# Top-32 attention and an ELU feed-forward layer: nine transposes of a step in a row, one GpSimd operation for both rows' distances, and three-tile feed-forward blocks split into one and two tiles

## The chip, the core and the metric

The kernel runs on one core of a Trainium2 chip. The metric is the device time of one launch in microseconds (us), the median of several runs. A core has a matrix engine (TensorE, PE in the profile; PEld is its loading of weights), VectorE (DVE), ScalarE (ACT), GpSimd (POOL) and a queue that issues DMAs (SyncE, SP). Each engine takes its instructions in program order, and instructions of different engines wait for each other by semaphores.

## The reference

```python
scores = scale * np.matmul(q, k.transpose(0, 1, 3, 2))      # 8 batches, 8 heads, 576 x 576, head_dim 64
kth = np.partition(scores, -top_k, axis=-1)[..., -top_k:-top_k + 1]   # top_k = 32
scores = np.where(scores >= kth, scores, -1000000000.0)
scores = scores - np.max(scores, axis=-1, keepdims=True)
attn = np.exp(scores)
attn = attn / (np.sum(attn, axis=-1, keepdims=True) + 1e-09)
attn_out = np.matmul(attn, v)
# (B,H,S,D) -> (B*S, H*D): x has 4608 tokens of 512
h = x @ w_in                                                 # 512 -> 2048
g = np.where(h > 0.0, h, np.exp(np.minimum(h, 0.0)) - 1.0)
out = g @ w_out                                              # 2048 -> 512
```

So there are two parts: attention in which each query keeps its 32 largest scores, and a feed-forward layer (FFN) on the tokens that come out of it. All of it is computed in fp32.

## The kernel before

**Steps.** The 576 queries of a batch are four tiles of 128 and a remainder of 64. A step is one query tile with a pair of heads ("two rows": head i=0 and i=1, each 128 queries by 576 keys); for the remainder it is 64 queries with four heads. There are 18 steps in a batch, 144 in all. In an even batch the order is tiles (0,1), tiles (2,3), remainder; in an odd batch the remainder comes first, so that the remainders of a pair of batches, which together fill one tile of 128 tokens, follow each other. The first eight steps (`n < tight`) are ordered by a scheduler, while the weights are still being decoded; from step 8 on the order is the one written out in the main loop (L702 to L755), which in step n works on four steps at once:

- at its head the score matmuls of step n+2 (`scores`, matmuls at L331; ScalarE copies them out at L339), then the attention matmuls of a group of two steps that has all its transposes (`attend`, L470, with the copy to the FFN's input `xT` at L497);
- in four parts, the selection of step n on VectorE (`select`: `max` at L373 and L385, `match_replace` at L378), 14 passes of 576 elements over two rows;
- between the parts, for step n-1: the distance of the 32nd score from the largest on GpSimd (L406), and on ScalarE a Prelu and an Exp that leave exp(score - largest) for the kept scores and 0 for the others (`mask`, L407 and L408, row 0 after the first part, row 1 after the second); after the fourth part the division by the sum on GpSimd (`normalise`, L418 to L425);
- for step n-2: nine 128x128 transposes on TensorE (`turn`, L444) with three copies by ScalarE (L445). `main` (chunks 0 to 3) and `rest` (chunk 4, which holds parts of both rows) come after the second part, `other` (chunks 5 to 8) after the third;
- four times in a step `feed(n, 0.25)` puts in pieces of the FFN.

`turn(done, main)` needs row 0 of `normalise`, `rest` and `other` need row 1. `main` and `other` each take one of two PSUM buffers of `ps_t`, which `attend` uses too; `rest` uses a corner of the scores' own PSUM tile.

**FFN blocks.** Tiles of a pair of batches are put together to blocks of tokens (L604 to L613). The first pair has five blocks of one tile and two of two; each later pair has blocks (0,1), (2,3), (rest,4,5), (6,7), where `rest` is the tile of the two remainders. A block of s tiles has 16 pieces `hidden(f)` of four matmuls with 128·s columns (L545), then 4·s pieces `project` of four matmuls with 512 columns (L573). A `hidden` fills PSUM banks of 512 columns: one f for three tiles (384 of 512), two for two tiles, four for one. Each is evicted by two Relus (L555, L558), then an Exp and a copy on ScalarE (L560, L564), and an addition on GpSimd, or on VectorE in early steps and in the last block (`close_gates`, L515 and L517). An fp32 matmul of the program is two records in the profile.

**How much FFN a step gets.** A list `due` has for each block the step at which its input is ready (for a block, that of its last tile) and the planned cost of all blocks before it (`HIDDEN`, L21, per `hidden` by block size, and `PROJECT`). `feed` takes the smallest slope from what has been fed to any later entry of `due`:

```python
        ahead = [(w - fed["sum"]) / (x - fed["at"]) for x, w in due if x > fed["at"]]
        if ahead:
            fed["over"] += max(0.0, share * min(ahead))
        fed["at"] += share
        while ffn and decoded[0] >= ffn[0][1] and 0.5 * ffn[0][0] <= fed["over"]:
```

So the pace depends on steps and planned costs, not on the clock, and work is stretched to last until the next block is ready. What is left after step 146 is issued at the end (L756).

**VectorE's other work.** From the second batch on, VectorE transposes the queries and keys of a batch that comes next (L285, eight operations a batch) into a pool of five buffers (L116). A buffer comes free when the score matmuls that read it are done.

Of the kernel before, what the change touches and what calls it, by code (L numbers as in the profile page):

```python
# [9 lines left out]
ALU = mybir.AluOpType  # L10
FP32 = mybir.dt.float32
# [6 lines left out]
TAKEN = -1.0e30  # L18
EPS = 1.0e-9
STEEP = 2.0**96  # L20
HIDDEN = {1: 1.1, 2: 1.85, 3: 2.7}  # L21
PROJECT = 3.55


# [34 lines left out]
class Step:  # L59
# [7 lines left out]
    def __init__(self, t, hp, group, at):  # L67
        self.t, self.hp = t, hp
        self.group, self.at = group, at
        self.masked = self.normal = self.turned = False  # L70
        if t.rem:
            rows = [(4 * hp, 0), (4 * hp + 2, 0), (4 * hp + 3, 1), (4 * hp + 1, 1)]
            self.heads = [
                (h, i, slice(64 * (n % 2), 64 * (n % 2) + 64))
                for n, (h, i) in enumerate(rows)
            ]
        else:
            self.heads = [(2 * hp + i, i, slice(0, 128)) for i in range(2)]
# [3 lines left out]
def kernel(  # L82
# [9 lines left out]
    nc = tc.nc  # L92
    P = nc.NUM_PARTITIONS
    B, H, S, D = q.shape
    dm, dff = moe_w_in.shape[0], moe_w_in.shape[1] // 2
    J = S // P
# [4 lines left out]
    NC = dm // P  # L101
    NF = dff // P
    NG = NF // 2
    T = 3 * P
    KEYS, QUERIES = R, R + S
    Q = 32
    NB = S // Q
# [12 lines left out]
    small = pool("small", 4)  # L120
# [8 lines left out]
    early = raws.enter_context(tc.tile_pool(name="early", bufs=1))  # L129
# [236 lines left out]
    def select(u):  # L366

        u.first = small.tile([P, 2, 8], FP32, tag="m1", name="m1")
        u.last = small.tile([P, 2, 8], FP32, tag="m4", name="m4")
        cur = [u.sc[:, i, :] for i in range(2)]  # L370
        found = [u.first[:, i, :] for i in range(2)]
        for i in range(2):
            nc.vector.max(found[i], cur[i])  # L373
        yield
        wk = [wkpool.tile([P, S], FP32, tag=f"wk{i}", name="wk")[:] for i in range(2)]
        for r in range(TOP_K // 8 - 1):
            for i in range(2):
                nc.vector.match_replace(wk[i], found[i], cur[i], TAKEN)  # L378
            cur = wk
            for i in range(2):  # L380
                if r < TOP_K // 8 - 2:
                    found[i] = small.tile([P, 8], FP32, tag=f"m{i}", name="m")[:]
                else:
                    found[i] = u.last[:, i, :]
                nc.vector.max(found[i], cur[i])  # L385
            hook()
            yield

    def mask(u, i, early=False):

        if u.masked:
            return
        if i == 0:
            u.den = small.tile([P, 4], FP32, tag="den", name="den")
        u.masked = i == 1  # L400
        sc, low, top = u.sc[:, i, :], u.last[:, i, 7:8], u.first[:, i, 0:1]
        gap = u.den[:, 2 + i : 3 + i]
        if early:
            nc.scalar.activation(gap, top, AF.Prelu, scale=-1.0, bias=low, alpha=1.0)
        else:
            nc.gpsimd.tensor_tensor(gap, low, top, ALU.subtract)  # L406
        nc.scalar.activation(sc, sc, AF.Prelu, scale=-1.0, bias=low, alpha=1.0 / STEEP)  # L407
        nc.scalar.activation(  # L408
            sc, sc, AF.Exp, scale=-STEEP, bias=gap, accum_out=u.den[:, i : i + 1]
        )  # L410

    def normalise(u):
# [16 lines left out]
    def turn(u, chunks):  # L429

        if u.turned:
            return
        g = u.group
        if g.et is None:
            g.et = etpool.tile([P, 2 * J + 1, len(g.tiles), P], FP32, tag="et", name="et")
        if chunks.stop - chunks.start == 1:
            ps = wide[1][:, 1, HS : HS + P]
        else:
            ps = ps_t.tile([P, JP], FP32, tag="t", name="eps")
        sc = u.sc[:, :, :].rearrange("p i s -> p (i s)")  # L440
        n = chunks.stop - chunks.start
        for c in range(n):
            c0 = (chunks.start + c) * P
            nc.tensor.transpose(ps[:, c * P : (c + 1) * P], sc[:, c0 : c0 + P], ident[:])  # L444
        nc.scalar.copy(  # L445
            g.et[:, chunks, u.at, :],
            ps[:, 0 : n * P].rearrange("p (c q) -> p c q", c=n),
        )
        if chunks.stop == 2 * J + 1:
            u.turned = True  # L450
            if u.at == len(g.tiles) - 1:
                closing.append(g)
# [38 lines left out]
    def finish(blk, parts, at, cols, src):  # L491
        if blk.xT is None:
            if blk.slots == 1:
                blk.xT = xpool.tile([P, NC, P], FP32, tag="xT", name="xT")
            else:
                blk.xT = late["x"].tile([P, NC, T], FP32, tag="xT", name="xT")
        nc.scalar.copy(blk.xT[:, at, cols], src)  # L497
# [23 lines left out]
    def ffn_pieces(blk):  # L521
# [64 lines left out]

        part = HIDDEN[blk.slots]
        behind = 2 * NF if blk.number else 0
# [13 lines left out]
    for b in range(B):  # L602
        if b % 2 == 0:
            rest = 2 * J  # L604
            division = [(0,), (1,), (2,), (3,), (rest,), (4, 5), (6, 7)]
            if b > 0:
                division = [(0, 1), (2, 3), (rest, 4, 5), (6, 7)]
            slots = {}
            for part in division:
                blk = Block(len(blocks), len(part))  # L610
                blocks.append(blk)
                slots.update((x, (blk, s)) for s, x in enumerate(part))
        first[b] = len(steps)  # L613
        tiles = []
        for qt in range(J + 1):
            r0 = b * S + (JP if qt == J else qt if b == 0 else qt * P)
            if qt == J:
                (blk, slot), c0, n = slots[rest], (b % 2) * R, R
                rows = slice(r0, r0 + R)
            else:  # L620
                (blk, slot), c0, n = slots[(b % 2) * J + qt], 0, P
                rows = slice(r0, r0 + J * (P - 1) + 1, J) if b == 0 else slice(r0, r0 + P)
            c0 += slot * P
            t = Tile(b, qt, rows, blk, slice(c0, c0 + n))
            blk.left += NHP
            blk.tiles[slot].append(t)
            tiles.append(t)
        order = [(0, 1), (2, 3), (J,)] if b % 2 == 0 else [(J,), (0, 1), (2, 3)]
        if b == 0:
            order[:2] = [(0,), (1,), (2,), (3,)]  # L630
        for qts in order:
            for hp in range(NHP // 2 if qts == (J,) else NHP):
                group = Group([tiles[qt] for qt in qts], hp)
                steps += [Step(tiles[qt], hp, group, i) for i, qt in enumerate(qts)]
            for qt in qts:
                n = len(steps)
                tiles[qt].block.ready = n + 1.0 if n <= tight else n + 2.5
    NS = len(steps)
    total = 0.0
    for blk in sorted(blocks, key=lambda x: x.ready):  # L640
        due.append((blk.ready, total))
        total += NF * HIDDEN[blk.slots] + 4 * blk.slots * PROJECT

# [57 lines left out]
    main, rest, other = slice(0, J), slice(J, J + 1), slice(J + 1, 2 * J + 1)  # L701
    for n in range(NS + 3):  # L702
        for fn, args in todo.pop(n, []):
            fn(*args)
        ahead, cur, prev, done = step(n + 2), step(n), step(n - 1), step(n - 2)
        if n < tight:
            turn_qk(True)
            if n < 3:
                scores(ahead)
            if n > 1:  # L710
                scores(step(n + 3))
            for i in range(2):
                passes = select_row(cur, i, n < tight - 1)
                next(passes)
                if i == 0:
                    while closing:
                        attend(closing.pop(0))
                elif prev:
                    normalise(prev)
                    turn(prev, main)  # L720
                    turn(prev, rest)
                    turn(prev, other)
                feed(n, 0.25)
                next(passes)
                mask(cur, i, True)
                feed(n, 0.25)
            continue
        if n == tight:
            ctx.enter_context(tc.manual_schedule(engines=engines))
        passes = select(cur) if cur else iter(range(4))  # L730
        if ahead and n > tight:
            scores(ahead)
        while closing:
            attend(closing.pop(0))
        next(passes)
        feed(n, 0.25)
        if prev:
            mask(prev, 0)
        turn_qk()
        next(passes)  # L740
        feed(n, 0.25)
        if done:
            turn(done, main)
            turn(done, rest)
        if prev:
            mask(prev, 1)
        next(passes)
        feed(n, 0.25)
        if done:
            turn(done, other)  # L750
        next(passes)
        if prev:
            normalise(prev)
        feed(n, 0.25)
        turn_qk(True)  # L755
# [36 lines left out]
```

## Time and profile before

| what | us |
|---|---|
| runs shown | 1643.64, 1643.79, 1641.84; median 1643.64 |
| the profiled execution's own time | 1642.57 |
| its span, first to last instruction | 1640.8 |
| mean granted TensorE clock in it | 0.974 |
| busy: PE, PEld, DVE, ACT, POOL | 1581.7, 1011.8, 1453.4, 1187.7, 708.7 |

The profile is of one execution. Its page lists for each engine the busy time and its share of the span; a row of digits shows the busy share in tenths for each of 40 equal slices. Groups of instructions are named by line of the kernel, engine and operation, with what they write and read (`out<-in`), count, busy time and mean duration. "Idle before" is time in which the engine stood still just before such an instruction, with what ended it. The view of waits sums such idle time: who waited, for whom, total us, how often, the longest. The timeline lists instructions in order of time: start, duration of a merged run, engine, line, and in brackets the idle time before. Matmuls are pipelined, so that the duration of one (599 ns for 512 columns) is longer than the distance to the next.

### The profile page before, as it was taken

How to read it: one execution, taken by the hardware profiler on the slowest of the kernel's cores; microseconds unless marked ns; L12 is line 12 of the kernel's file. 1: busy time of each engine (PE TensorE's matmuls, PEld its weight loads, DVE VectorE, ACT ScalarE, POOL GpSimd, SP SyncE). 2: the span in 40 equal slices, each digit the busy share in tenths (PEclk: the TensorE clock that was granted, in tenths of full speed). 3: DMA queues.
4: the chain of work that ended last, by engine and by line, in shares of the span. 5: the costliest groups of instructions: out<-in, count | busy, mean ns of one | idle time of the engine just before them, and what ended most of it. 6: DMA issues, size and time to landing. Idle time of an engine off the chain costs nothing.

```text
span 1640.8 us, 25344 instructions
## 1 busy us (share of the span) xinstructions
PE 1581.7 (96%) x8276; PEld 1011.8 (62%) x8276; DVE 1453.4 (89%) x2981; ACT 1187.7 (72%) x2400; POOL 708.7 (43%) x1534
## 2 busy tenths in 40 slices
PE   4788999999999999999999999999999999999999
PEld 3566777666575757555566666655557575755564
DVE  6987999999999999999999699999999599998000
ACT  6887778778695867778678686868759595958521
POOL 4775445445353534445335353535435353534300
PEclk8579999999999999999999999999999999999999
DMA  7431221012100310012100211012100201000000
GB/s 226 151 128 25 50 40 26 7 22 45 42 1 7 59 42 8 7 22 44 36 14 15 43 30 28 1 28 44 36 14 0 43 1 35 1 13 2 7 13 14
DMA packets 188037, 56.18 MB, mean 34 GB/s; under 512 B 178177, under 2 KB 179201, under 8 KB 187905
## 3 DMA queue, kind: packets, MB, share of 16 engines
q1 hardware_dynamic: 186704, 54.26, 14.1%
q8 instruction: 66, 1.08, 0.3%
q14 instruction: 67, 0.54, 0.1%
q10 hardware_dynamic: 1200, 0.30, 0.1%
HBM read 45.09 MB, written 9.44 MB: 33 GB/s over the span
## 4 chain that ended last, share of the span: by engine, by line
PE 76%; ACT 12%; DVE 7%; POOL 3%; issue 1%; DMA 1%; SPq 0%; ACTq 0%; DVEq 0%; POOLq 0%
PE ops L573 29%; PE hps L545 23%; PE avps L470 10%; PE scps L331 7%; PE eps L444 6%; DVE wk L378 3%; DVE m L385 3%; ACT sc L408 2%; ACT et L445 2%; ACT sc L407 2%; DVE m L373 1%; ACT n L564 1%; ACT n L555 1%; ACT sc L339 1%; ACT n L560 1%
## 5 line engine op out<-in xcount | busy, mean ns | idle before, releaser
L385 DVE MAX8 m<-wk 128x8 f32<-128x576 f32 x816 | 577.9, 752 | 0.3 <-POOL den L406 0.3
L545 PE MATMUL hps<-xT,w_in 128*128 128x256 f32 (+2 forms) x2432 | 545.8, 374 | 0.0
L573 PE MATMUL ops<-w_out,gT 128*128 128x512 f32 x1152 | 523.6, 599 | 0.0
L545 PEld LDWEIGHTS hps<-xT,w_in 128*128 128x128 f32 x2432 | 406.0, 192 | 100.1 <-issue 26.3
L378 DVE MATCH_REPLACE8 wk<-m,wk 128x576 f32<-128x576 f32 x544 | 401.4, 748 | 0.0
L573 PEld LDWEIGHTS ops<-w_out,gT 128*128 128x128 f32 x1152 | 209.0, 190 | 233.9 <-issue 232.8
L418 POOL TENSOR_SCALAR dene<-den 128x2 f32<-128x2 f32 x144 | 32.9, 228 | 686.5 <-ACT sc L408 686.1
L408 ACT ACTIVATE sc<-sc,den 128x576 f32<-128x576 f32 x288 | 223.6, 776 | 65.5 <-POOL den L406 44.2
L407 ACT ACTIVATE sc<-sc,m 128x576 f32<-128x576 f32 x288 | 225.3, 782 | 10.8 <-DVE m L385 10.7
L470 PE MATMUL avps<-et,vT 128*64 128x256 f32 (+2 forms) x2080 | 207.2, 330 | 17.4 <-ACT et L445 17.2
L425 POOL TENSOR_SCALAR sc<-sc,rec 128x576 f32<-128x576 f32 x288 | 213.0, 750 | 15.0 <-POOL rec L423 0.2
L331 PE MATMUL scps<-kqT 64*128 64x288 f32 (+1 forms) x1280 | 206.0, 442 | 13.6 <-ACT kqT L307 9.1
L339 ACT ACTIVATE sc<-scps 128x576 f32<-128x576 f32 x288 | 171.8, 647 | 65.1 <-PE scps L331 65.1
L445 ACT COPY et<-eps 128x512 f32<-128x512 f32 x288 | 164.6, 571 | 73.4 <-PE eps L444 73.4
L378 DVE MATCH_REPLACE8 wk<-m,sc 128x576 f32<-128x576 f32 x272 | 200.6, 748 | 0.0
L373 DVE MAX8 m<-sc 128x8 f32<-128x576 f32 x272 | 191.6, 749 | 8.8 <-ACT sc L339 8.8
L444 PEld LDWEIGHTS eps<-ident,sc 128*128 128x128 f32 x1152 | 144.9, 144 | 87.2 <-issue 52.7
L444 PE MATMUL eps<-ident,sc 128*128 128x128 f32 x1152 | 177.1, 279 | 13.7 <-POOL sc L425 13.7
L470 PEld LDWEIGHTS avps<-et,vT 128*64 128x64 f32 x2080 | 128.5, 142 | 98.8 <-ACT et L445 31.7
L515 POOL TENSOR_TENSOR gT<-n,gT 128x512 f32<-128x512 f32 (+1 forms) x119 | 164.9, 1386 | 31.2 <-ACT n L564 31.1
L331 PEld LDWEIGHTS scps<-kqT 64*128 64x128 f32 (+1 forms) x1280 | 111.3, 182 | 89.5 <-issue 43.8
L555 ACT ACTIVATE n<-hps 128x512 f32<-128x512 f32 (+1 forms) x156 | 87.3, 559 | 56.8 <-PE hps L545 56.0
(53 smaller groups left out, 1089.6 us busy)
## 6 DMA issues: line engine op xcount, KB each, us to landing
raw<-in_moe_w_in_dram SPq DMA_DIRECT2D x16, 512.0 KB, 6.1
vT<-in_v_dram SPq DMA_DIRECT2D x64, 128.0 KB, 2.5
raw<-in_moe_w_out_dram SPq DMA_DIRECT2D x16, 512.0 KB, 3.6
out_dram<-osb SPq DMA_DIRECT2D x32, 256.0 KB, 2.1
kin<-in_k_dram SPq DMA_DIRECT2D x112, 72.0 KB, 2.5
qin<-in_q_dram SPq DMA_DIRECT2D x112, 72.0 KB, 2.6
kin<-in_k_dram SPq DMA_DIRECT2D x8, 128.0 KB, 4.5
vT<-in_v_dram SPq DMA_DIRECT2D x64, 16.0 KB, 2.2
```

The lines of the kernel that those rows point to most:

```text
L331: nc.tensor.matmul(wide[i][rows, half, 0:HS], kq[part, q0 : q0 + u.t.ql], kq[part, k0 : k0 + HS], start=True, stop=True,)
L373: nc.vector.max(found[i], cur[i])
L378: nc.vector.match_replace(wk[i], found[i], cur[i], TAKEN)
L385: nc.vector.max(found[i], cur[i])
L407: nc.scalar.activation(sc, sc, AF.Prelu, scale=-1.0, bias=low, alpha=1.0 / STEEP)
L408: nc.scalar.activation(sc, sc, AF.Exp, scale=-STEEP, bias=gap, accum_out=u.den[:, i : i + 1])
L425: nc.gpsimd.tensor_scalar(u.sc[:, i, :], u.sc[:, i, :], rec[:, i : i + 1], 1.0, ALU.mult, ALU.mult)
L444: nc.tensor.transpose(ps[:, c * P : (c + 1) * P], sc[:, c0 : c0 + P], ident[:])
L445: nc.scalar.copy(g.et[:, chunks, u.at, :], ps[:, 0 : n * P].rearrange("p (c q) -> p c q", c=n),)
L470: nc.tensor.matmul(ps[i * D : (i + 1) * D, cols], vt[:, 2 * J + i if c == J else i * J + c, :], w, start=(c == 0), stop=(c == J),)
L545: nc.tensor.matmul(blk.h[:, f % bank, :], w_in[:, i, f * P : (f + 1) * P], blk.xT[:, i, 0:n_tok], start=(i == 0), stop=(i == NC - 1),)
L573: nc.tensor.matmul(blk.o[:], blk.gT[f // NG][:, f % NG, s * P : (s + 1) * P], w_out[:, f, :], start=(f == 0), stop=(f == NF - 1),)
```

## The change

It has three parts.

1. In the main loop `turn(done, other)` moves from after the third part of the step to between `main` and `rest`, so that the nine transposes are issued together, and the three copies on ScalarE before the mask of row 1.
2. The two GpSimd subtractions of one column (L406, one for each row) become one of two columns, `distance`, at the very head of the step, before the scores and any FFN piece. It waits for the last `max` of both rows. In the first eight steps the distance stays on ScalarE.
3. The block (rest, 4, 5) of the later pairs becomes two: (rest,) and (4, 5). `T`, the width of the FFN's buffers, falls from 384 to 256 tokens.

```diff
-HIDDEN = {1: 1.1, 2: 1.85, 3: 2.7}
+HIDDEN = {1: 1.1, 2: 1.85}
...
+        self.left = 9
...
-    T = 3 * P
+    T = 2 * P
...
-        if i == 0:
+        if i == 0 and early:
             u.den = small.tile([P, 4], FP32, tag="den", name="den")
...
         if early:
             nc.scalar.activation(gap, top, AF.Prelu, scale=-1.0, bias=low, alpha=1.0)
-        else:
-            nc.gpsimd.tensor_tensor(gap, low, top, ALU.subtract)
         nc.scalar.activation(sc, sc, AF.Prelu, scale=-1.0, bias=low, alpha=1.0 / STEEP)
...
+    def distance(u):
+
+        if u.masked:
+            return
+        u.den = small.tile([P, 4], FP32, tag="den", name="den")
+        nc.gpsimd.tensor_tensor(
+            u.den[:, 2:4], u.last[:, :, 7], u.first[:, :, 0], ALU.subtract
+        )
...
-        if chunks.stop == 2 * J + 1:
+        u.left -= n
+        if u.left == 0:
             u.turned = True
...
-                division = [(0, 1), (2, 3), (rest, 4, 5), (6, 7)]
+                division = [(0, 1), (2, 3), (rest,), (4, 5), (6, 7)]
...
+        if prev:
+            distance(prev)
         passes = select(cur) if cur else iter(range(4))
         if ahead and n > tight:
             scores(ahead)
...
         if done:
             turn(done, main)
+            turn(done, other)
             turn(done, rest)
         if prev:
             mask(prev, 1)
         next(passes)
         feed(n, 0.25)
-        if done:
-            turn(done, other)
         next(passes)
```

## The prediction

> **What bounds the kernel now.** I read the page first, then the busy time by stretch, then the waits, then the timeline of TensorE.
>
> ```profile
> PE 1581.7 (96%) x8276; PEld 1011.8 (62%) x8276; DVE 1453.4 (89%) x2981; ACT 1187.7 (72%) x2400; POOL 708.7 (43%) x1534
> PE   4788999999999999999999999999999999999999
> DVE  6987999999999999999999699999999599998000
> ```
>
> Two engines are full, TensorE to the end and VectorE until about 1520 us. They can't both set the pace. The stretches tell them apart:
>
> ```profile
> core 0: us, PE busy (x) PEld busy (x) DVE busy (x) ACT busy (x) POOL busy (x), PEclk, DMA share, GB/s
> 200.00:400.00 200.00, 194.50 (x1346) 139.83 (x1345) 200.00 (x412) 156.34 (x318) 91.69 (x212) 0.99 0.13 27
> 400.00:600.00 200.00, 196.31 (x1020) 123.87 (x1019) 200.00 (x412) 149.57 (x302) 90.04 (x207) 1.00 0.14 27
> ...
> 800.00:1000.00 200.00, 200.00 (x1071) 126.82 (x1070) 185.77 (x384) 145.22 (x293) 83.82 (x197) 1.00 0.13 28
> ...
> 1200.00:1400.00 200.00, 200.00 (x1109) 129.78 (x1109) 178.69 (x368) 146.24 (x296) 84.28 (x195) 1.00 0.08 19
> ```
>
> Up to 600 VectorE has no idle moment and TensorE stands still for 4 to 5 us in 200. From 800 on it is the other way round: TensorE never stops and VectorE does. The waits say for what:
>
> ```profile
> DVE kqT L285 <- PE scps L331: 32.3, 3, 16.9
> ...
> ACT sc L408 <- POOL den L406: 44.2, 49, 4.3
> ...
> PE avps L470 <- ACT et L445: 17.2, 21, 3.3
> PE eps L444 <- POOL sc L425: 13.7, 5, 4.3
> ```
>
> VectorE lost 32.3 us at three transposes of new keys, because the score matmuls that free the buffer came late: TensorE had fallen behind by that much. So the end is set by how much TensorE has to do, and by the few times it stood still after it became the later one.
>
> That "busy" is true work must be shown, since durations of pipelined matmuls overlap. The distance from one run of matmuls to the next does it:
>
> ```profile
> 262.15 1.06 PE L545 MATMUL hps<-xT,w_in 128*128 128x128 f32 x8
> 263.04 0.60 PE L444 MATMUL eps<-ident,sc 128*128 128x128 f32 x4
> ...
> 269.28 2.94 PE L545 MATMUL hps<-xT,w_in 128*128 128x128 f32 x24
> 272.06 0.60 PE L444 MATMUL eps<-ident,sc 128*128 128x128 f32 x4
> ```
>
> Eight matmuls of 128 columns took 263.04 - 262.15 = 0.89 us, 111 ns each (116 in the run of 24, which begins behind another kind). In the same way 256 columns took 216 ns (1032.67 to 1034.40, eight), 384 took 323 (1103.05 to 1105.64, eight), 512 about 429 (823.07 to 826.51, eight), a transpose 109. These are 0.84 to 0.87 ns a column. Nothing is left between them in the full stretches.
>
> **The split block.** A block of three tiles has 16 x 4 multiplications of 384 columns, two records each: 128 x 323 ns = 41.3 us. One tile and two tiles make 128 x (111 + 216) = 41.9 us. With 112 and 322, the values that occur most, the difference is 128 x 6 ns = 0.77 us a pair of batches, **+2.3 us** for the three pairs. Bounds: with 116 for the narrow form +3.8, with 111 and 323 +1.5. The 512-column projections don't change. ScalarE's evictions are 29.1 us before (32 x 0.486 and 16 x 0.845) and 29.4 after (24 operations of 0.593 and 24 of about 0.63), GpSimd's additions 8 x 1.82 against 12 x 1.28: both engines have 25% and more to spare.
>
> On this the Trainium skill speaks against the change. "TensorE: Matmul & The Clock Gate", section "Back-to-back issue gap", gives for a stream of weight loads and matmuls 81 ns at 128 columns and 131 at 512, so a narrow matmul costs much more per column; on a straight line the split would cost 64 ns for each of 384 pairs, 24.7 us, and by it the sum would end near 1660. The rows above show time in proportion to columns, and they decide.
>
> **Where the FFN goes.** The split has a second effect. Before, the entry in the list of due times after block (2,3) is that of (rest,4,5), eight steps after the remainders are done. With a block of its own, the remainder tile is due eight steps sooner and the slope to that entry is steeper. I added up the FFN matmuls in the order of both built programs with the distances above: ahead of the scores of step 36 they come to 161 us before and 163 after, of step 45 to 216 and 227, of step 57 to 289 and 309, of step 89 to 502 and 530, of the last step to 879 and 901. All of it is 994 and 996. So up to 28 us of FFN come earlier, most from steps 36 to 57, and behind the last scores 20 us less is left. That is no gain by itself: the work is pulled into stretches in which TensorE is already 98% busy. It makes TensorE the later engine from about step 40 (400 us) on instead of step 55 to 60. The last steps stay covered: between the last scores and the last transposes TensorE still has 28 multiplications of 0.43 us, 24 of 0.86 and two attentions of 2.5, about 38 us, while VectorE needs 9.6 for the step, ScalarE and GpSimd some 6.
>
> **Transposes together.** Nine transposes and three copies stay what they were. What goes is a wait: the attention at the next step's head needs the copy of `other`, which stood on ScalarE behind the mask of row 1 and any FFN eviction. From 390 us on TensorE waited so:
>
> ```profile
> PE avps L470 <- ACT et L445: 7.0, 11, 1.2
> PE scps L444 <- ACT sc L339: 1.8, 4, 0.6
> ```
>
> The copy now comes a half step before the attention. Since TensorE is then the later engine, no other wait takes its place: **-7.0 us**. The 1.8 us are transposes of `rest` that come before row 1 is normalised; I leave them. At 148.32 the same wait is 2.34 us, behind two weight conversions; it delays an FFN piece whose Exp holds up VectorE for 5.74 us at 162.40, in the stretch that VectorE paces. The transposes after that attention (150.64) could start 1.86 sooner, as row 0 was normalised at 148.78, less the 0.57 by which the mask comes later: **-1.3 us**, bounds 0 and -2.3. Between 200 and 390 TensorE waits 3.3 us for these copies, but VectorE paces there: 0, at best -3.3.
>
> The added cost: ScalarE's mask of row 1 stands behind one more copy, 0.57 us, and behind the mask is `normalise`, and behind that the next transposes. At 1032.12 this chain is: transposes, copy at 1034.49, mask to 1036.77, GpSimd from 1036.95 to 1040.40, 8.3 us in all, and the next transposes at 1041.38, 9.26 after the first. The margin is 0.98; the change takes 0.57 of it, and `other` asks for row 1 0.44 after the first transpose. So it holds in stretches of 9.2 us and more: 0.
>
> **The distances.** Of 272 subtractions of 0.19 us half go, 26 us of GpSimd, off the path. ScalarE's 44.2 us of waiting, mostly for a subtraction queued behind an addition of 1.28 us, should nearly vanish. Queued behind the new operation, which waits for VectorE's last `max`, are GpSimd's FFN additions, needed a half step later or more. Row 0's Exp now waits for row 1's last `max` as well, at most 0.75 us, less than the margin above. ScalarE was not what TensorE waited for in these places, so 0; bounds -1.8 (the waits of `rest` go) and +1.8.
>
> **Sum.** +2.3 - 7.0 - 1.3 = -6.0 us on the profiled execution's 1642.57, so 1636.6. The median of the runs shown is 1.07 above it: **1637.6**. A measurement can tell about 0.2% (3.3 us) from no change.
>
> **Rivals.**
> *More than that.* If TensorE had real room early, 20 us less work behind the last scores would show in full, 1643.6 + 2.3 - 20 = 1626. Against it: its idle time from 200 to 800 is 5.5 + 3.7 + 2.9 = 12 us. I allow all of the waits, -3.3 and -1.8 besides the sum: 1632.5. Chance 0.13.
> *VectorE paces for longer.* If TensorE gets behind only at step 55 as before, about half of the 7.0 lies where VectorE sets the time, and the early wait may be replaced by one for GpSimd's `normalise`: +2.3 - 3.5 = -1.2, 1642.4. For it: VectorE is at 200 of 200 until 800. Against it: 20 us of FFN is more than the 12 us of idle. Chance 0.18.
> *The third copy makes TensorE wait for* `normalise`*.* By the built order, from step 34 on 11 stretches between transposes are only 7.4 to 7.8 us of matmuls (5 before), because FFN pieces fall unevenly. There the chain of 8.3 + 0.57 exceeds 7.5 + 0.44 by 0.9 us. If ScalarE is as late in all as at 1034.49, that is +10 us: 1637.6 + 10 = 1648, slower. It decides from seven stretches on (6 / 0.9). Against it: nine of the 11 follow a stretch of projections, which leave ScalarE free, and there (1094.99) the copy started after 0.68 us and the chain was 6.6. Chance 0.14.
>
> **How the numbers follow.** Forecast 0.55, the three rivals 0.13, 0.18, 0.14. Faster by over 0.2%: 0.52 + 0.13 = 0.65; within: 0.03 + 0.18 = 0.21; slower 0.14. The range runs from a bit below the first rival, for the ends of the split's and the early wait's price, to the last: 1631 to 1648.
>
> **What would show it.** Right: no 384-column matmul, 128-column ones still at 111 to 116 ns; the attention's wait for the copies gone; ScalarE's wait for the distance nearly gone; VectorE idle at key transposes already near step 50; its end later, and less FFN behind it, with the span shorter only by the waits. Wrong: TensorE waiting for GpSimd's `normalise` at transposes beyond 400 us, 128-column matmuls spaced wider, or TensorE idle in the last 100 us because too little FFN is left.

## The result, and the profile after

| | before | after |
|---|---|---|
| median, us | 1643.72 (4 runs, 1641.84 to 1644.53) | 1618.60 (4 runs, 1617.99 to 1620.59) |
| profiled execution, us | 1642.57 | 1617.99 |
| its span, us | 1640.8 | 1616.2 |
| mean granted TensorE clock | 0.974 | 0.974 |

The ratio is 0.9853 [0.9839, 0.9868]: faster by 25 us, where 6 were forecast. The time lies 12 us below the range.

The page of the changed kernel: busy times, and the rows of tenths for TensorE and VectorE.

```profile
PE 1572.3 (97%) x8660; PEld 1049.6 (65%) x8660; DVE 1451.6 (90%) x2981; ACT 1189.1 (74%) x2400; POOL 693.5 (43%) x1410
PE   5889999999999999999999999999999999999999
DVE  6988999999999999999999599999999879999500
```

TensorE has 384 records more (the narrow matmuls) and is busy 9.4 us less, in a span that is 24.6 us shorter. VectorE's row ends one slice later only because the slices are shorter: its last step starts at about the same time, as is shown below. By stretch of 200 us, with the columns of the table before:

```profile
200.00:400.00 200.00, 196.57 (x1324) 140.59 (x1323) 200.00 (x414) 157.49 (x319) 90.27 (x190) 0.98 0.13 26
400.00:600.00 200.00, 200.00 (x998) 125.59 (x997) 196.68 (x405) 145.46 (x293) 81.50 (x176) 1.00 0.14 28
800.00:1000.00 200.00, 199.94 (x1081) 132.48 (x1079) 179.72 (x371) 148.98 (x300) 83.82 (x176) 1.00 0.13 27
1200.00:1400.00 200.00, 200.00 (x1149) 135.14 (x1147) 181.19 (x373) 154.58 (x312) 88.37 (x181) 1.00 0.07 17
```

From 400 us on TensorE has no idle moment and VectorE has some, which before came only from 800 on (from 600 to 800 VectorE was busy for 200.00 us and TensorE for 197.14). The waits of the changed kernel, largest that concern the change:

```profile
DVE kqT L286 <- PE scps L332: 37.3, 4, 16.8
...
ACT sc L407 <- POOL den L416: 18.8, 16, 3.2
...
PE eps L452 <- POOL sc L433: 12.9, 7, 3.8
...
PE scps L332 <- ACT et L453: 3.3, 3, 2.7
PE avps L479 <- ACT et L453: 3.0, 2, 2.5
```

The attention's wait for the copies fell from 17.2 to 3.0 us, ScalarE's for the distance from 44.2 to 18.8. From 390 us on the changed kernel shows no wait of TensorE at all, where the old one shows 8.8 us (7.0 and 1.8). All this is as forecast, and explains 9 of 25 us at most.

**Where the 24.6 us went.** TensorE never rests for long, so I took from both traces the time from the start of each matmul record to the start of the next, whatever lies between, and summed it by kind of the first. Idle time and slow matmuls are both in it.

| kind | before, us | after, us | difference |
|---|---|---|---|
| attention (`avps`) | 216.7 | 184.0 | -32.7 |
| transposes of a step | 157.6 | 149.9 | -7.7 |
| `hidden` | 530.6 | 532.6 | +2.0 |
| `project` | 505.1 | 509.8 | +4.7 |
| scores | 203.6 | 212.3 | +8.7 |
| transposes before the steps | 17.2 | 17.8 | +0.6 |

The attention has the same 2080 records in both. From 390 us on the 50 attentions of two steps take 2.70 us each before and 2.31 after; with the distance from the record before them, which holds any idle time ahead of the first one, 3.03 and 2.65. That is 50 x 0.38 = 19 us lost, where the waits of the same stretch showed 7.0. About 12 of the 32.7 us lie before 390 us; of that stretch, VectorE has no idle moment from 200 us on.

How 7.0 can stand for 19 is seen in one place of the **old** kernel's timeline (start, duration, then the instruction; GpSimd, VectorE and weight loads left out):

```profile
646.98 0.57 ACT L555 ACTIVATE n<-hps 128x512 f32<-128x512 f32 x1
...
647.46 0.58 ACT L558 ACTIVATE gT<-hps 128x512 f32<-128x512 f32 x1
647.93 0.63 ACT L560 ACTIVATE n<-n 128x512 f32<-128x512 f32 x1
648.14 0.65 PE L470 MATMUL avps<-et,vT 128*64 128x256 f32 x2
648.59 0.63 ACT L564 ACTIVATE n<-n 128x512 f32<-128x512 f32 x1
649.13 0.57 ACT L445 COPY et<-eps 128x512 f32<-128x512 f32 x1
...
649.75 2.37 PE L470 MATMUL avps<-et,vT 128*64 128x256 f32 x18 [0.96 <-ACT et L445]
652.05 1.13 PE L545 MATMUL hps<-xT,w_in 128*128 128x256 f32 x4
```

ScalarE works off four evictions of an FFN piece before it comes to the copy of `other` (L445). TensorE's first attention matmul (two records) reads only the copy of `main` and runs at 648.14; the second needs the copy. The records of an attention normally start in twos, the two heads side by side on 64 columns each: in the changed kernel's attention below the second record of a pair starts 6 to 7 ns after the first, the next pair some 210 ns later. Here the first matmul runs alone, its second record 267 ns after its first, and the profile counts idle time only from its modelled end: 0.96 us. From 648.14 to the next kind at 652.05 it is 3.91 us against 2.31, so 1.60 are lost. The **changed** kernel, a step of the same stretch:

```profile
652.75 1.05 ACT L453 COPY et<-eps 128x512 f32<-128x512 f32 x2
653.70 0.28 ACT L453 COPY et<-scps 128x128 f32<-128x128 f32 x1
...
655.91 2.38 PE L479 MATMUL avps<-et,vT 128*64 128x256 f32 x20
...
658.22 1.98 PE L582 MATMUL ops<-w_out,gT 128*128 128x512 f32 x4
```

All three copies are done 2 us before the attention, whose 20 records run in one go: 658.22 - 655.91 = 2.31.

The second half of the account is the end. VectorE begins its last step at 1510 us before and at 1509 after. Behind that there were 1640.8 - 1510 = 131 us, and now 107. The FFN that the program leaves behind the last scores is 114.4 us before and 94.7 after (the built orders, with the distances of the prediction). So what TensorE won did not make VectorE earlier: it was filled with 20 us of FFN that formerly came last.

### The profile page after: what moved, and what is told of

Read it like the earlier page. It is cut to its first block, busy times and chain, and to the rows that moved or that the text cites. A ratio compares the mean times of both kernels' runs of the same rounds, so it can differ in the third digit from the quotient of the medians.

```text
span 1616.2 us, 25917 instructions
## 1 busy us (share of the span) xinstructions
PE 1572.3 (97%) x8660; PEld 1049.6 (65%) x8660; DVE 1451.6 (90%) x2981; ACT 1189.1 (74%) x2400; POOL 693.5 (43%) x1410
## 4 chain that ended last, share of the span: by engine, by line
PE 85%; ACT 6%; DVE 4%; POOL 2%; issue 1%; DMA 1%; SPq 0%; ACTq 0%; POOLq 0%
PE ops L582 30%; PE hps L554 28%; PE avps L479 9%; PE scps L332 9%; PE eps L452 7%; ACT sc L407 1%; DVE wk L379 1%; ACT et L453 1%; DVE m L386 1%; PE scps L452 1%; ACT sc L406 1%; DVE wk L355 1%; DVE m L361 1%; POOL sc L433 0%; ACT sc L340 0%
## 5 line engine op out<-in xcount | busy, mean ns | idle before, releaser
L386 DVE MAX8 m<-wk 128x8 f32<-128x576 f32 x816 | 654.2, 940 | 0.0
L554 PE MATMUL hps<-xT,w_in 128*128 128x256 f32 (+1 forms) x2816 | 541.8, 347 | 0.0
L554 PEld LDWEIGHTS hps<-xT,w_in 128*128 128x128 f32 x2816 | 454.4, 193 | 68.9 <-issue 25.1
L379 DVE MATCH_REPLACE8 wk<-m,wk 128x576 f32<-128x576 f32 x544 | 452.2, 936 | 0.0
L407 ACT ACTIVATE sc<-sc,den 128x576 f32<-128x576 f32 x288 | 224.0, 778 | 34.9 <-POOL den L416 18.8
L406 ACT ACTIVATE sc<-sc,m 128x576 f32<-128x576 f32 x288 | 226.3, 786 | 6.2 <-DVE m L386 6.2
L379 DVE MATCH_REPLACE8 wk<-m,sc 128x576 f32<-128x576 f32 x272 | 225.3, 930 | 0.0
L374 DVE MAX8 m<-sc 128x8 f32<-128x576 f32 x272 | 216.6, 932 | 5.5 <-ACT sc L340 5.5
L524 POOL TENSOR_TENSOR gT<-n,gT 128x512 f32<-128x512 f32 x131 | 167.3, 1277 | 78.3 <-ACT n L573 78.3
L479 PE MATMUL avps<-et,vT 128*64 128x256 f32 (+2 forms) x2080 | 186.1, 326 | 3.0 <-ACT et L453 3.0
L452 PE MATMUL eps<-ident,sc 128*128 128x128 f32 x1152 | 155.9, 278 | 13.2 <-POOL sc L433 12.9
L379 DVE MATCH_VALUE_LOAD wk<-m,wk 128x8 f32 x544 | 146.9, 270 | 0.0
```

Of the source, the lines that this page charges most:

```text
L407: nc.scalar.activation(sc, sc, AF.Exp, scale=-STEEP, bias=gap, accum_out=u.den[:, i : i + 1])
L479: nc.tensor.matmul(ps[i * D : (i + 1) * D, cols], vt[:, 2 * J + i if c == J else i * J + c, :], w, start=(c == 0), stop=(c == J),)
L554: nc.tensor.matmul(blk.h[:, f % bank, :], w_in[:, i, f * P : (f + 1) * P], blk.xT[:, i, 0:n_tok], start=(i == 0), stop=(i == NC - 1),)
```

## The experiments

**Theory:** the cost taken away is the lateness of the copy of `other` behind FFN evictions on ScalarE, about three times its recorded idle time. It makes room on TensorE, and the split block's steeper slope fills that room. **Rivals:** the broken pairs of matmuls, not the lateness, are what is lost; the split block brings the gain by itself, by pulling FFN forward; the distances bring it. Each ratio below is to the old kernel on the same chip.

### Each part alone

Part 1, transposes together (and the counter `u.left`):

```diff
             turn(done, main)
+            turn(done, other)
             turn(done, rest)
...
         feed(n, 0.25)
-        if done:
-            turn(done, other)
         next(passes)
```

> The kernel before with the nine transposes together and nothing else. Theory P (pairs): the 20 records of a two-step attention run two at a time; where the second one has to wait for the copy of `other`, the pairs shift and the first two and the last two records run alone, so that an attention takes about 2.85 us and not 2.31, waits included. Then this edit alone makes every attention 2.31, and the time falls by most of the 32.8 us that attention lost, less what lies in steps that VectorE paces: 1622 to 1632. Theory R (room): the gain came from the FFN work that the split pulls ahead, into idle time of TensorE that the waits did not show. Then this edit alone gives no more than the 7.0 + 1.3 us that were forecast: 1635 to 1638. Theory D (distances): ScalarE's 44 us of waiting for GpSimd were on the path; then nothing here: 1641 to 1645.

1632.79 us, 0.9937 [0.9923, 0.9950]. The time of the attentions, start to start, is 184.2 us, just as in the changed kernel: so the whole -32.5 comes from this part. Yet the time falls only by 10 us (0.0063 x 1644). The waits of this kernel show where a part of the rest is:

```profile
PE eps L445 <- POOL sc L426: 18.3, 12, 3.6
...
PE scps L332 <- ACT et L446: 8.8, 9, 2.7
```

TensorE, ahead now, waits at transposes for `normalise` (13.7 us before), which comes at the end of a step's chain from VectorE on, and at scores for ScalarE's copies. From 390 us on these are 1.6 and 3.8 us. Start to start the scores take 220.8 us, 17.2 more than before.

Part 2, the distances in one operation at the step's head (`distance` as in the change, and the subtraction at L406 taken out):

```diff
+        if prev:
+            distance(prev)
         passes = select(cur) if cur else iter(range(4))
```

> The kernel before with the two distances in one GpSimd operation at the step's head and nothing else. P and R: within 2 us of the kernel before, 1641 to 1646, attentions still at 2.7 us on average. D: most of the 25 us, 1618 to 1630.

1641.41 us, 0.9982 [0.9972, 0.9993]: about 3 us faster. Attentions of two steps take 2.67 us from 390 us on, the wait for the copies is 15.2 us instead of 17.2, and ScalarE's wait for the distance is 44.3, not less. So part 2 isn't the cause of the gain, and alone it doesn't do what I thought it would.

Part 3, the split block:

```diff
-HIDDEN = {1: 1.1, 2: 1.85, 3: 2.7}
+HIDDEN = {1: 1.1, 2: 1.85}
...
-    T = 3 * P
+    T = 2 * P
...
-                division = [(0, 1), (2, 3), (rest, 4, 5), (6, 7)]
+                division = [(0, 1), (2, 3), (rest,), (4, 5), (6, 7)]
```

> The kernel before with the block of three tiles split into one and two and nothing else. P: the copies are as late as before, attentions stay at 2.6 to 2.8 us; 2.3 us more work for TensorE, a few us gained where it stood idle: 1639 to 1647. R: FFN work moves into idle time, 1620 to 1630. D: 1643 to 1647.

1668.85 us, 1.0153 [1.0138, 1.0169]: 25 us **slower**. The wait of its attentions, and one place of its timeline:

```profile
PE avps L470 <- ACT et L445: 39.6, 32, 2.7
```

```profile
841.91 0.58 ACT L555 ACTIVATE n<-hps 128x512 f32<-128x512 f32 x1
...
842.39 0.59 ACT L558 ACTIVATE gT<-hps 128x512 f32<-128x512 f32 x1
842.86 0.63 ACT L560 ACTIVATE n<-n 128x512 f32<-128x512 f32 x1
843.06 0.65 PE L470 MATMUL avps<-et,vT 128*64 128x256 f32 x2
843.52 0.63 ACT L564 ACTIVATE n<-n 128x512 f32<-128x512 f32 x1
844.06 0.57 ACT L445 COPY et<-eps 128x512 f32<-128x512 f32 x1
...
844.68 2.37 PE L470 MATMUL avps<-et,vT 128*64 128x256 f32 x18 [0.97 <-ACT et L445]
```

The same picture as before, more often. From 390 us on, 21 of the 50 attentions of two steps wait for a copy that stands behind four evictions, and nearly all that is lost is lost there (39.9 of 40.7 us); in the kernel before it is 10 of the 50, behind two or four. The 50 take 3.12 us on average. The rival "the split brings the gain by itself" falls.

### Is it the pairs or the lateness?

The old kernel, with the second head's matmul first in the attention, so that nothing can start before the copy of `other`:

```diff
-                for i in range(2):
+                for i in (1, 0):
```

> The kernel before with the two heads exchanged in the attention's inner loop, so that the matmul that reads the copy of `other`, the late one, is the first of the 20 records and not the second pair's partner. Nothing else moves: the copy is as late as before. P: TensorE waits as long or a little longer at the attention, but the pairs stay whole, so the attention's own records come back to 2.31 us and 10 to 16 us of the gain appear without any of the change's three parts: 1628 to 1634. R and D: nothing, or slower, since TensorE now stands still before the first record: 1643 to 1650.

1645.24 us, 1.0012 [1.0002, 1.0021]. In the same step as above:

```profile
648.31 1.24 PE L331 MATMUL scps<-kqT 64*128 64x288 f32 x8
...
650.48 0.57 ACT L445 COPY et<-eps 128x512 f32<-128x512 f32 x1
...
651.10 2.38 PE L470 MATMUL avps<-et,vT 128*64 128x256 f32 x20 [1.54 <-ACT et L445]
653.41 1.35 PE L545 MATMUL hps<-xT,w_in 128*128 128x256 f32 x5
```

The attention runs whole, 2.31 us, and its wait is recorded in full: 1.54 us here. Over the run the wait grows from 17.2 to 29.9 us, and from 390 us on from 7.0 to 19.3, which is the 19 worked out above:

```profile
PE avps L470 <- ACT et L445: 19.3, 24, 1.8
```

With the wait an attention takes 3.08 us, with the broken pairs 3.03. So mending the pairs wins nothing while the copy is late: the lateness is the loss, and the old profile recorded a third of it. What the broken pairs do is to make the head start worthless: after the copy the old order still took 652.05 - 649.75 = 2.30 us for its 18 records, as long as all 20 take in pairs. The pairing theory falls as an explanation of the change.

A broken pair does cost when nothing is late. The changed kernel, with each attention's first matmul ahead of the scores of the step's head and the others behind them:

(`attend` gets an argument for this, which isn't shown:)

```diff
...
+        for g in closing:
+            attend(g, True)
         if ahead and n > tight:
             scores(ahead)
         while closing:
             attend(closing.pop(0))
```

> The changed kernel with the first matmul of each attention ahead of the step's scores and the other nine behind them, so that it runs without its partner though no copy is late. It is the cost of the broken pairs without any waiting. If a record that runs alone costs its full time, an attention is longer by about 0.54 us, the first and the last two records alone (2.85 against 2.31): 56 attentions of 20 records and 16 of the smaller form, 1635 to 1648. If the recorded pattern costs nothing, 1617 to 1621.

1649.54 us, 1.0044 [1.0031, 1.0057]; the changed kernel again on the same chip:

> The changed kernel once more, beside the others on the same chip: 1617 to 1621.

1619.97 us, 0.9867 [0.9851, 0.9882]. So the order costs 29.6 us, with no more waiting (`avps` 4.3 us in all). A step of e10:

```profile
901.90 0.65 PE L484 MATMUL avps<-et,vT 128*64 128x256 f32 x2
902.47 1.24 PE L333 MATMUL scps<-kqT 64*128 64x288 f32 x8
903.64 2.37 PE L484 MATMUL avps<-et,vT 128*64 128x256 f32 x18
905.95 3.70 PE L590 MATMUL ops<-w_out,gT 128*128 128x512 f32 x8
```

0.57 us for the first matmul and 2.31 for the nine others, 2.88 together, against 2.31 for all ten: the first without its partner costs its time, and the others are paired one off, so that the last runs alone too (its two records start 215 ns apart, and nothing starts beside them). Start to start, attentions take 221.1 us against 183.6.

### What makes the copy late

The changed kernel with the transposes still together on TensorE, and only ScalarE's copy of `other` put off until after the mask and the third feed (`turn` gets an argument that keeps the copy in the list `waiting`; that part isn't shown):

```diff
...
-            turn(done, other)
+            turn(done, other, waiting)
...
         feed(n, 0.25)
+        while waiting:
+            waiting.pop(0)()
         next(passes)
```

> The changed kernel with the nine transposes together on TensorE as they are, but ScalarE's copy of `other` put back to where it stood, after the mask of row 1 and the third FFN feed. L: the place on ScalarE is all that matters: attentions next to `hidden` pieces take 3.9 to 4.5 us again, 1650 to 1672, near the split alone (1668.9). Rival T (transposes in a row are what helps TensorE): 1618 to 1625.

1664.68 us, 1.0138 [1.0125, 1.0151], 45 us more than the changed kernel:

```profile
PE avps L485 <- ACT et L454: 40.0, 34, 4.0
```

This is near the split alone (1.0153 [1.0138, 1.0169]). So that the transposes stand together on TensorE is worth nothing that can be told from it; what counts is the place of one copy of 0.57 us in each step on ScalarE. Then the transposes and the copy of `other` behind the mask of row 1, but ahead of the third feed:

```diff
             turn(done, main)
-            turn(done, other)
             turn(done, rest)
         if prev:
             mask(prev, 1)
         next(passes)
+        if done:
+            turn(done, other)
         feed(n, 0.25)
```

> The changed kernel with the transposes and the copy of `other` put back behind the mask of row 1, but ahead of the third FFN feed, so that only the mask and not the FFN's evictions stands ahead of the copy. If the evictions make the copy late (L's finer form): attentions at 2.31 us, 1617 to 1623. If the mask's 1.75 us alone are enough to make it late: 1640 and more.

1616.78 us, 0.9849 [0.9836, 0.9861], as fast as the changed kernel (0.9853 and 0.9867), with one wait for the copy from 390 us on:

```profile
PE avps L479 <- ACT et L453: 0.4, 1, 0.4
```

Its attentions take 191.3 us start to start, 7 more than the changed kernel's, but most of that lies before 390 us and doesn't show in the time. So with the FFN paced as in the changed kernel, it is the evictions of the third feed that make the copy late, not the mask; in e7 all of the 37 us that attentions of two steps lose from 390 us on are lost behind four evictions. In the kernel before this is only half of it: 10.3 of its 19.7 us are lost where evictions stand between mask and copy, and 9.3 where none do and the mask (at the very end a copy of the output) is directly ahead. There the transposes of `other` also come only after the third feed, so that less matmul work lies between them and the attention; the two were not taken apart. This is the fastest kernel measured; the intervals don't tell it from the changed one.

### What the split adds

The changed kernel without part 3 (the three lines of e3 taken back):

```diff
-                division = [(0, 1), (2, 3), (rest,), (4, 5), (6, 7)]
+                division = [(0, 1), (2, 3), (rest, 4, 5), (6, 7)]
```

> The changed kernel with the blocks of three tiles kept: transposes together and distances together, FFN in the order and amounts of the kernel before. The theory by now, L: a late copy of `other` costs TensorE 20 to 40 us in all, far more than its recorded idle time; freed of it, TensorE runs ahead of VectorE in the first half and stands still there unless FFN work is pulled forward, which the split does. By L this kernel is 10 us or more above the changed one: 1627 to 1632 (1632.8 of the transposes alone, less about 2.5 for the distances). Rival S (the split brings nothing of its own once the copy is early): 1616 to 1621, as it saves 2.3 us of matmuls.

1628.79 us, 0.9918 [0.9905, 0.9931]. The split is worth 8 to 11 us on top (to 0.9867 or 0.9853), where it cost 25 alone. To tell its matmuls from its pace, the changed kernel with the split kept, but the list of due times giving the old pace step by step (ahead of the scores of steps 45, 57 and the last 216, 289 and 882 us of FFN, against 216, 289 and 879 before):

```diff
-    for blk in sorted(blocks, key=lambda x: x.ready):
-        due.append((blk.ready, total))
+    order = sorted(blocks, key=lambda x: x.ready)
+    alone = [x.slots == 1 and x.number > 6 for x in order]
+    for i, blk in enumerate(order):
+        if alone[i]:
+            due.append((order[i + 1].ready, total))
+        elif not (i and alone[i - 1]):
+            due.append((blk.ready, total))
```

> The changed kernel with one edit: in the list of due times the remainder's block has the due time that the block of three tiles had, so that the pace of the FFN is the old one, step by step, while the matmuls are those of the split (one and two tiles). L: the gain of the split is its pace; without it 2.3 us slower than the kernel without the split, 1629 to 1635. Rival F (the forms bring it: fuller PSUM banks and shorter evictions): as the changed kernel, 1617 to 1621.

1628.99 us, 0.9924 [0.9911, 0.9936], like e5. So the gain of the split is its pace, and what its narrow matmuls cost is too small to be told at the end (the intervals overlap). By stretch, e6:

```profile
200.00:400.00 200.00, 195.53 (x1356) 140.38 (x1355) 200.00 (x412) 158.83 (x321) 91.21 (x195) 0.99 0.13 27
400.00:600.00 200.00, 197.48 (x1023) 124.74 (x1022) 200.00 (x412) 147.54 (x300) 86.58 (x186) 1.00 0.15 29
600.00:800.00 200.00, 198.92 (x1135) 135.01 (x1134) 200.00 (x413) 156.29 (x317) 87.83 (x190) 1.00 0.14 29
```

At the old pace VectorE has no idle moment until 800 us, and TensorE shows waits again: 18.4 us for `normalise` in the whole run against 12.9 in the changed kernel, and from 390 us on 3.6 in all where the changed kernel has none. By this the room that the punctual copies make can't be used there: without more FFN to do, TensorE is held to VectorE's pace. VectorE's last step starts at 1500 us in e6 and e1, but 129 us of work remain behind it; in the changed kernel it starts at 1509 and 107 remain.

### What the distances add

The changed kernel without part 2 (`distance` taken out, and two subtractions of one column again, in `mask`):

```diff
-        if prev:
-            distance(prev)
         passes = select(cur) if cur else iter(range(4))
```

> The changed kernel with the two distances put back, one of one column at each mask. Both theories that are left: the distances are worth 0 to 4 us, as they were on the kernel before: 1617 to 1623. ScalarE's wait for GpSimd's distance goes back from 19 to 40 us and more.

1620.19 us, 0.9868 [0.9855, 0.9882], against 0.9867 for the changed kernel beside it. ScalarE's wait for the distance is 29.4 us instead of 18.8, and costs nothing. Without the split part 2 seems worth about 3 us (e1 to e5, 0.9937 to 0.9918, intervals overlapping; e2). Why there and not here was not tried.

| parts | ratio | us, by the ratio |
|---|---|---|
| 1 | 0.9937 | -10 |
| 2 | 0.9982 | -3 |
| 3 | 1.0153 | +25 |
| 1 and 2 | 0.9918 | -13 |
| 1 and 3 | 0.9868 | -22 |
| 1, 2 and 3 | 0.9853, 0.9867 | -24, -22 |

## Why the prediction was wrong in size

**The step that failed first: "-7.0 us".** The prediction took TensorE's recorded idle time before the attentions from 390 us on as what the late copies cost. The mechanism and its sign were right, the size was not: start to start the loss there is 19 us (50 x 0.38), and e4 makes the record itself show it, 19.3. The prediction had the rows to see it: it checked by start-to-start distance that `hidden`, `project` and transposes lose nothing, but did not do it for the attention, the one group it was about to price. "Nothing is left between them" was true for the kinds measured and taken for all. The Trainium skill ("Perfetto Trace Analysis", section "Optimization Strategy") advises to look for the gaps between slices on the limiting engine and for what blocks it there; the gaps led to the right place, and here held a third of the loss.

**The second, which weighs more: "That is no gain by itself: the work is pulled into stretches in which TensorE is already 98% busy."** By itself it is even a loss of 25 us (e3), because the pulled pieces bring evictions that stand ahead of the copy. Together with part 1 it is a gain of 8 to 11 (e5, e6), where the sum had +2.3. The 98% counted the late attentions as busy, and their loss (32.7 us in the whole run) became room when part 1 took it away. Part 1 alone turned only a part of that room into time: 10 us (e1), where -7.0 and -1.3 were forecast. So most of the 19 us that the forecast missed are the split's, in room that the first error hid. The parts were priced one by one and added; they can't be, as -10 and +25 give -22.

**The rivals.** "More than that" came nearest. It named what happened, less work behind the last scores that shows "in full", on the condition that TensorE "had real room early"; but its 1626 lies 7 us above the result, and without part 1 there was no such room (e3). It was given 0.13, with the reason that idle time from 200 to 800 us is only 12 us: the same misreading as above. "VectorE paces for longer" is what e6 shows at the old pace; in the changed kernel TensorE is full from 400 us on. The third copy made TensorE wait for nothing: there is no wait for `normalise` from 390 us on, and all such waits are 12.9 us against 13.7. That cost of 0 held.

**The split block's matmuls: right by their spacing.** Forecast +2.3 us, bounds +1.5 and +3.8. From 390 us on the medians from record to record are 112 and 216 ns where 323 was before, so 128 x 5 ns = 0.64 us a pair of batches, +1.9 in all. The sums of `hidden`, start to start, can't confirm so small a term: they grew by 2.0 from before to after and by 3.8 from e5 to e6, whose pace is the same, but also by 5.3 from before to e1, where no matmul changed. A row of the changed kernel:

```profile
698.34 2.94 PE L554 MATMUL hps<-xT,w_in 128*128 128x128 f32 x24
701.12 1.04 PE L452 MATMUL eps<-ident,sc 128*128 128x128 f32 x8
```

(701.12 - 698.34) / 24 = 116 ns for 128 columns, the upper bound used. By the estimate from the Trainium skill that was weighed there ("TensorE: Matmul & The Clock Gate", section "Back-to-back issue gap") the split would have cost 24.7 us; for these fp32 matmuls this is not borne out.

**The early wait, -1.3: not settled.** VectorE starts step 16 at 214 us before, and at 210 and 213 in two profiles of the changed kernel. The two differ by more than the term.

**The distances, 0 within 1.8: right** for the changed kernel (e9), a little short for the part alone (e2). The reason was partly wrong: the wait "should nearly vanish", but stayed at 44.3 us in e2 and at 18.8 in the changed kernel.

**What would show it.** The matmul widths, the vanished wait for copies and VectorE's idle time at key transposes near step 50 (3.3 us in the stretch from 400) came as said. "Its end later" did not: VectorE's last step starts when it did. And the span became shorter by far more than "only by the waits". The tail stayed covered, as the end of the changed kernel's TensorE timeline shows:

```profile
1551.27 2.38 PE L479 MATMUL avps<-et,vT 128*64 128x256 f32 x20
1553.58 3.70 PE L582 MATMUL ops<-w_out,gT 128*128 128x512 f32 x8
1557.11 27.79 PE L554 MATMUL hps<-xT,w_in 128*128 128x256 f32 x128
1584.74 27.63 PE L582 MATMUL ops<-w_out,gT 128*128 128x512 f32 x64
```

## What to carry to other kernels

Price a stall by the time from a group's start to the start of what follows it, against the group's best case, not by its recorded idle time: an engine that can begin part of the group hides the rest of the stall. Look for small copies that stand on an engine behind another job's evictions, since such a copy can set the pace of the largest engine (0.57 us of ScalarE in each step, moved, were 45 us here). Work pulled forward pays only where the limiting engine has room, so price it together with the part that makes the room.

## What the runs showed of the hardware

- The two attention matmuls on 64 columns each run side by side: 20 records in 2.31 us, and 2.88 with the first matmul put elsewhere (e10). An order that shifts the pairs by one cost 29.6 us in the whole run, without more waiting in the profile.
- Durations of VectorE differ from profile to profile at the same pace: its second to fourth `max` passes (`m<-wk`) have a mean of 752 ns in the profile before, of 940 ns in the one after, and of 747 ns when the changed kernel was run again (e11), while a step of 14 passes takes 9.62 to 9.64 us in all three where VectorE is full. A duration from one profile is no cost; the distance to the next instruction is.
